# A weight stream issued from two engines instead of one

## The chip, the cores and the metric

The kernel runs on one core of a Trainium2 chip. The metric is device time in microseconds (us) of one execution. Time before the change: 2597.24 us, the median of 3 runs (2592.43 to 2603.32).

## The reference, cut to what matters

All arrays are bf16. Two branches are mixed by a gate per row: `A` is a recurrent attention with memory over 64 segments, `B` is a gated feed-forward block.

```python
# x: 2048 x 1024; 32 heads of 128; memory of 8 rows; segments of 32 rows
mem = mem0
for s in range(64):
    h = concat([mem, x[32 * s:32 * s + 32]])            # 40 rows
    q, k, v = h @ Wq, h @ Wk, h @ Wv                    # each 1024 x 4096
    scores = where(mask, q @ k.T * scale, -1e9)         # by head, 40 x 40
    o = softmax(scores) @ v
    o = o @ Wo                                          # 4096 x 1024
    mem = o[:8]                                         # goes into the next segment
    outs.append(o[8:])
a = concat(outs)
b = (gelu(x @ w_gate) * (x @ w_up)) @ w_down            # inner width 3584
g = sigmoid((x * gate_w).sum(-1))
out = g * a + (1 - g) * b
```

A segment needs the memory rows of the one before, so the 64 segments follow each other. Each uses all four attention weights, 8 MB apiece, and SBUF does not hold all of them.

## The kernel before, in words

**Recording and order.** The kernel records operations with `op(engine, function, r, w, dsem)`. Each engine (pe, act, dve, pool, sp) then runs its own operations strictly in the order in which they were recorded. `_Sched` derives the waits from what is read (`r`) and written (`w`), and `lower` turns them into semaphore waits. An operation that must wait stops its engine's queue at that point; everything recorded later on that engine stands behind it. A DMA is an operation of the engine that issues it, and it raises its own semaphore (`dsem`) when it has landed.

**First part, up to 603 us.** Branch B runs in four blocks of 512 rows; its results go to a DRAM scratch (`b_scr`). In the same time 19 pieces of 512 KB of the attention weights are rearranged in DRAM into `w_scr` (`copy_wide`), each as 128 rows of 4 KB.

**Recurrent part, the 64 segments.** Most of the attention weights stay in SBUF (`arena`), some pieces are kept in PSUM banks or in small buffers and copied back in each segment (lines 870 to 881), and 19 pieces a segment come anew from `w_scr`: the weight stream. They go through `ring`, which has 10 slots of 256 KB. A piece takes two slots, so the ring holds five blocks. Because the first segment has one block of a single slot, later blocks begin at odd slots, and each fifth block wraps around the end of the ring and is loaded by two DMAs of 256 KB.

`stream` lists the blocks in the order of their use. `stream_next` records the load of the next block, on SP. It is called by `slot_free`, which stands right behind the PE operations that use up a block: recorded there, the load waits for those matmuls, since it overwrites the slots that they read. SP does nothing else in this part.

In a segment PE projects q, k and v for two halves of the heads (line 894, eight steps a projection, four matmuls of 512 columns a step, two of the eight steps from the ring), transposes q and k (line 921), forms scores (954), transposes the probabilities (984), multiplies them by v (995) and applies the output projection (1036). Rows that can be computed ahead for four later segments run in between (795 and 1017).

ACT, in its order: it evicts q and k (`rows`, line 900), evicts rows computed ahead (`rowsx`, 809), takes the exponential of the softmax (967, behind DVE's subtraction at 965), copies v (`vt`, 914), one of the transposes (926), the attention output (`oT` and `oe`, 1003 and 1004), and at the end of a segment the output rows (`rows`, 1129). That last copy leads over one PE transpose (1137) and one DVE copy (`hT`, 1142) to the memory rows of the next segment. POOL issues the small loads and stores (x, the rows computed ahead, v rows, b, the output) from a queue of its own.

Of the kernel before, what the change touches and what calls it, by code (L numbers as in the profile page):

```python
# [26 lines left out]
class _Sched:  # L27
# [10 lines left out]
    def op(self, eng, mk, r=(), w=(), dsem=None):  # L38
        o = _Op(eng, mk, dsem)
        deps = []  # L40
        if eng == "pool" and dsem is None:
            w = [*w, ("pool",)]
        for k in r:
            deps += self.w.get(k, ())
            if k[0] == "P":
                deps += [x for x in self.r.get(k, ()) if x.eng != eng]
        for k in w:
            deps += self.w.get(k, ())
            deps += self.r.get(k, ())
        for k in r:  # L50
            self.r.setdefault(k, []).append(o)
        for k in w:
            self.w[k] = [o]
            self.r[k] = []
        seen = set()
        for d in deps:
            if d is o or id(d) in seen:
                continue
            seen.add(id(d))
            if d.eng == eng and d.dsem is None and (eng == "pe" or eng == "sp"):  # L60
                continue
            o.deps.append(d)
            d.sig = True
        self.ops.append(o)
        return o
# [63 lines left out]
def bass_gated_mix__memory_aug_recurrent_mem_tr__geglu_ffn__prompt_kernel(  # L129
# [38 lines left out]
    with ExitStack() as es:  # L168
# [54 lines left out]
        op = g.op  # L223
# [353 lines left out]
        n_str = [0]  # L577
        at = [0]

        def stream_next():  # L580
            s, u, wd = stream[n_str[0]]
            n_str[0] += 1
            sl = at[0]
            at[0] = (sl + wd) % RING
            slots = [(sl + j) % RING for j in range(wd)]
            for j in range(wd):
                slot_of[(s, u, j)] = slots[j]
            if u in wide:
                src = w_scr[wide.index(u), :, 0:wd * 1024]
            else:  # L590
                src = A_Wq[u[2] * 128:(u[2] + 1) * 128, 16 - 8 * wd if wd == 2 else 8:16, :].rearrange("p h e -> p (h e)")
            cut = min(wd, RING - sl)
            for a, b in ((0, cut), (cut, wd)):
                if a < b:
                    op("sp", lambda e, a=a, b=b: e.dma_start(
                        ring[:, slots[a]:slots[a] + b - a, :].rearrange("p a b -> p (a b)"), src[:, a * 1024:b * 1024]),
                       r=[("rp", u)], w=[("ring", y, x) for y in slots[a:b] for x in range(2)], dsem=f"ring{slots[a]}")

# [2 lines left out]
        def slot_free(k):  # L601
            free[0] += k
            while n_str[0] < len(stream) and free[0] >= stream[n_str[0]][2]:
                free[0] -= stream[n_str[0]][2]
                stream_next()
# [601 lines left out]
```

## Time and profile before

| | before |
|---|---|
| median of 3 runs | 2597.24 us |
| profiled execution | 2594.39 us |
| its span, first to last instruction | 2592.6 us |
| PE busy | 2288.7 us (88%) |
| DVE busy | 1213.1 us (47%) |
| ACT busy | 881.8 us (34%) |
| POOL busy | 546.0 us (21%) |
| mean granted TensorE clock | 0.966 |
| moved by DMA | 797.27 MB |
| of it through SP's hardware queue (q1) | 737.31 MB |
| through ACT's hardware queue (q10) | 0.06 MB |
| through POOL's software queue (q0) | 54.99 MB |
| ring loads, all issued by SP | 973 of 512 KB, 486 of 256 KB, and two from `A_Wq` |

The span is what lies between the first and the last instruction of the profiled execution, whose own time is 1.8 us longer. Busy times leave out instructions that issue DMAs, wait or branch. A share of the whole span mixes the first part, where branch B is computed, with the recurrent part, so the views by window and by wait say more on the stream than the totals do. Where a wait has several causes, the profile names the last one.

### The profile page before, as it was taken

The numbers are of one execution on the slowest core, as the hardware profiler recorded it, in microseconds if no ns is written. First come the engines' busy times: TensorE is split into PE (matmuls) and PEld (weight loads), VectorE is DVE, ScalarE is ACT, GpSimd is POOL, SyncE is SP. The second block draws the span as 40 slices with busy tenths as digits, with TensorE's granted clock in tenths as the row PEclk, the third lists the DMA queues.
The fourth block names the chain that finished last, engine by engine and source line by source line (L and its number), as shares of the span: only waits on it lengthen the run. The fifth ranks groups of instructions, "written<-read, shape, count | busy, mean of one in ns | idle before, by whom it ended". The sixth has DMA issues, their size and how long they took to land.

```text
span 2592.6 us, 77055 instructions
## 1 busy us (share of the span) xinstructions
PE 2288.7 (88%) x33919; PEld 1141.8 (44%) x33975; DVE 1213.1 (47%) x3497; ACT 881.8 (34%) x2131; POOL 546.0 (21%) x908
## 2 busy tenths in 40 slices
PE   8999999998888888888888888888888888988887
PEld 4444444444444444444444444444444444444444
DVE  5626262533444444445544444545444444455444
ACT  3314131321333333333333333333333333333332
POOL 1000003001222222222322222222222222223222
PEclk9999999999899999999999899999998999999988
DMA  8627263567999999999999999999999999999998
GB/s 286 223 75 261 75 205 97 179 247 258 331 318 343 345 348 354 355 340 369 361 357 356 339 349 336 356 323 366 354 346 335 354 335 365 345 368 357 357 344 286
DMA packets 325533, 797.27 MB, mean 308 GB/s; under 512 B 54552, under 2 KB 112232, under 8 KB 324432
## 3 DMA queue, kind: packets, MB, share of 16 engines
q1 hardware_dynamic: 282544, 737.31, 79.2%
q0 software_dynamic: 42512, 54.99, 6.8%
q8 instruction: 267, 4.37, 0.7%
q14 instruction: 66, 0.54, 0.1%
q10 hardware_dynamic: 144, 0.06, 0.0%
HBM read 764.52 MB, written 37.22 MB: 309 GB/s over the span
## 4 chain that ended last, share of the span: by engine, by line
PE 61%; DMA 26%; DVE 7%; issue 2%; ACT 2%; POOL 0%; SPq 0%; DVEq 0%; ACTq 0%
DMA ring<-w_scr 24%; PE pbb L894 10%; PE pba L894 9%; PE pbc L795 4%; PE pbb L1036 3%; PE pba L1036 3%; PE pbe L984 2%; PE pbe L921 2%; DVE ptb L989 2%; PE pbe L445 2%; PE pbh L445 2%; PE pbf L445 2%; PE pbg L445 2%; PE pbc L1017 2%; PE pbf L995 2%
## 5 line engine op out<-in xcount | busy, mean ns | idle before, releaser
L894 PE MATMUL pbb<-arena,hT 128*32 128x512 bf16 x4416 | 380.4, 399 | 9.1 <-DVE hT L1142 9.1
L894 PE MATMUL pba<-arena,hT 128*32 128x512 bf16 x4416 | 374.3, 390 | 8.8 <-DVE hT L1142 8.8
L928 DVE COPY qk<-pbe 128x512 bf16<-128x512 bf16 x192 | 132.9, 692 | 417.6 <-PE pbe L921 417.6
L967 ACT ACTIVATE pbd<-pbd 104x160 f32<-104x160 f32 x256 | 71.9, 281 | 514.3 <-DVE pbd L965 514.3
L703 POOL DMA_DIRECT2D vt<-v_scr x252 | 144.9, 577 | 335.1 <-PE pbf L995 199.5
L795 PE MATMUL pbc<-arena,xe 128*32 128x512 bf16 x2208 | 192.4, 385 | 9.7 <-DVE pn L1154 8.4
L989 DVE COPY ptb<-pbe 80x320 bf16<-80x320 bf16 x256 | 81.9, 320 | 251.5 <-PE pbe L984 251.5
L894 PE MATMUL pbb<-ring,hT 128*32 128x512 bf16 x1536 | 160.8, 407 | 29.8 <-DMA ring<-w_scr 28.9
L894 PE MATMUL pba<-ring,hT 128*32 128x512 bf16 x1542 | 157.4, 395 | 33.6 <-DMA ring<-w_scr 32.2
L894 PEld LDWEIGHTS pbb<-arena,hT 128*32 128x32 bf16 x4416 | 121.5, 100 | 120.7 <-issue 20.8
L894 PEld LDWEIGHTS pba<-arena,hT 128*32 128x32 bf16 x4416 | 119.7, 98 | 114.0 <-DVE hT L1142 14.6
L900 ACT ACTIVATE rows<-pba 128x512 bf16<-128x512 f32 x128 | 76.6, 598 | 244.5 <-PE pba L894 244.5
L1036 PE MATMUL pba<-arena,oT 128*32 128x256 bf16 x2176 | 136.0, 289 | 21.4 <-ACT oT L1003 19.0
L1036 PE MATMUL pbb<-arena,oT 128*32 128x256 bf16 x2176 | 139.9, 283 | 12.0 <-ACT oT L1003 11.7
L690 POOL DMA_DIRECT2D qkst<-qk_scr x126 | 71.8, 570 | 355.4 <-DVE qk L940 355.4
L974 DVE TENSOR_TENSOR pn<-pbd,rr 104x256 bf16<-104x256 f32 (+1 forms) x512 | 142.3, 319 | 8.8
L1036 PE MATMUL pba<-ring,oT 128*32 128x256 bf16 x1792 | 117.0, 284 | 29.4 <-DMA ring<-w_scr 28.1
L1003 ACT ACTIVATE oT<-pbf 128x256 bf16<-128x256 f32 x256 | 97.7, 382 | 131.4 <-PE pbf L995 131.4
L900 ACT ACTIVATE rows<-pbb 128x512 bf16<-128x512 f32 x128 | 76.6, 598 | 190.4 <-PE pbb L894 190.4
L1036 PE MATMUL pbb<-ring,oT 128*32 128x256 bf16 x1792 | 123.2, 280 | 15.3 <-DMA ring<-w_scr 13.1
L968 DVE TENSOR_REDUCE rs<-pbd 104x4 f32<-104x160 f32 x256 | 82.9, 324 | 88.9 <-ACT pbd L967 88.9
L961 DVE SCALAR_TENSOR_TENSOR pbd<-pbd,mask 104x160 f32<-104x160 f32 x256 | 85.2, 333 | 76.0 <-PE pbd L954 76.0
(245 smaller groups left out, 4257.7 us busy)
## 6 DMA issues: line engine op xcount, KB each, us to landing
ring<-w_scr SPq DMA_DIRECT2D x973, 512.0 KB, 6.3
ring<-w_scr SPq DMA_DIRECT2D x486, 256.0 KB, 5.9
arena<-in_B_w_gate_dram SPq DMA_DIRECT2D x28, 1024.0 KB, 5.4
arena<-in_B_w_up_dram SPq DMA_DIRECT2D x28, 1024.0 KB, 7.8
qkst<-qk_scr POOLq DMA_DIRECT2D x126, 64.0 KB, 5.2
qk_scr<-rowsx POOLq DMA_DIRECT2D x60, 128.0 KB, 5.2
arena<-in_B_w_down_dram SPq DMA_DIRECT2D x7, 1024.0 KB, 12.3
arena<-in_A_Wk_dram SPq DMA_DIRECT2D x6, 1024.0 KB, 6.6
```

Source lines behind the costliest of these rows:

```text
L445: ins = e.matmul(PB[bank][:, :], lhsT=wv[:, kc, col:col + 128], rhs=xb[:, kc, :], start=(kc == 0), stop=(kc == KC - 1))
L703: op("pool", lambda e: e.dma_start(vt[2 * SEG:KEYS, par, :], src), r=[("vscr", s // GR, h)], w=[("vte", par), ("vte", par, 0)], dsem="vte% ...
L795: ins = e.matmul(PB[B_X][32 * gq:32 * gq + 32, :], lhsT=xe[:, us[-1], :], rhs=us[gq // 2][0][gq % 2], start=(n == 0), stop=(n == KC - 1), ...
L894: ins = e.matmul(PB[bank][32 * gq:32 * gq + 32, :], lhsT=hT[:, kc, :], rhs=us[gq // 2][0][gq % 2], start=(x == 0), stop=(x == KC - 1), ski ...
L900: op("act", lambda e: e.activation(rows[:, :], PB[bank][:, :], ACTF.Copy), r=[P(bank)], w=[("rows",)])
L928: op("dve", lambda e: e.tensor_copy(qk[:, m, :, 0:SEG, :], src), r=[P(B_T)], w=[("qk", m)])
L961: op("dve", lambda e: e.scalar_tensor_tensor(out=sv, in0=sv, scalar=scale, in1=mask[0:104, None, :].to_broadcast([104, 4, L]), op0=ALU.mul ...
L968: op("dve", lambda e: e.tensor_reduce(rsv, sv, AX.X, ALU.add), r=[P(B_S)], w=[("rs",)])
L974: op("dve", lambda e, c0=c0, k0=k0, n=n: e.tensor_tensor(out=pn[0:104, :, c0:c0 + 2 * n].rearrange("p i (two c) -> p i two c", two=2), in0 ...
L989: op("dve", lambda e: e.tensor_copy(ptb[0:KEYS, :, :, :], src), r=[P(B_PT)], w=[("ptb",)] + first)
L1003: op("act", lambda e: e.activation(dst, src[:, :, :, 0:SEG], ACTF.Copy), r=[P(B_PV)], w=[("oT", o % 2)])
L1036: ins = e.matmul(PB[B_O][32 * q:32 * q + 32, 0:256], lhsT=oT[:, o % 2, k, :], rhs=u[q // 2][:, (q % 2) * 256:(q % 2 + 1) * 256], start=(o ...
```

## The change

One line is added and one changed in `stream_next`. From the second segment on (`s > 0`), a block whose number in the stream is odd is issued by ACT (`nc.scalar`), an even one by SP. `n_str[0]` has been raised by one before this line, so blocks count from one. Both DMAs of a split block are issued by the same engine. The waits, the slots, the order in which the loads are recorded and the semaphores that tell of their landing stay; the loads of ACT take their places in ACT's own order, right behind the operations recorded before them.

```diff
             cut = min(wd, RING - sl)
+            eng = "act" if s > 0 and n_str[0] % 2 else "sp"
             for a, b in ((0, cut), (cut, wd)):
                 if a < b:
-                    op("sp", lambda e, a=a, b=b: e.dma_start(
+                    op(eng, lambda e, a=a, b=b: e.dma_start(
                         ring[:, slots[a]:slots[a] + b - a, :].rearrange("p a b -> p (a b)"), src[:, a * 1024:b * 1024]),
                        r=[("rp", u)], w=[("ring", y, x) for y in slots[a:b] for x in range(2)], dsem=f"ring{slots[a]}")
```

Line numbers in the text are those of the kernel before; from line 594 on the changed kernel's are higher by one.

## The prediction

> **What bounds the kernel now.** I read the windows view first, to see which resources are full in the recurrent stage, where all the moved transfers lie. Its columns are: window, length, then busy time and instructions of PE, PEld, DVE, ACT and POOL, the granted TensorE clock, the DMA share and GB/s.
>
> ```profile
> 1000.00:1500.00 500.00, 432.14 (x8098) 223.74 (x8099) 239.29 (x791) 183.40 (x454) 130.74 (x213) 0.98 0.98 353
> 1500.00:2000.00 500.00, 428.96 (x7880) 219.48 (x7872) 237.88 (x789) 181.05 (x449) 126.65 (x207) 0.96 0.97 347
> 2000.00:2500.00 500.00, 430.05 (x7964) 220.57 (x7966) 239.75 (x792) 183.36 (x455) 126.38 (x207) 0.97 0.99 354
> ```
>
> Two things are nearly full at once: the DMA engines carry packets for 0.97 to 0.99 of the time, and PE is busy for 0.86. ACT is busy for 0.37, so it has room. Line 1142 runs 50 times from 1006.3 to 2495.8 us: 49 steps, 30.4 us a segment. The change acts on 63 of the 64 segments, some 1,915 us.
>
> Next the waits of PE, whole span (total us, times, longest):
>
> ```profile
> PE pba L894 <- DMA ring<-w_scr: 32.2, 51, 1.8
> PE pbb L894 <- DMA ring<-w_scr: 28.9, 52, 2.3
> PE pba L1036 <- DMA ring<-w_scr: 28.1, 39, 1.8
> PE pbe L1137 <- ACT rows L1129: 23.5, 48, 0.5
> PE pba L1036 <- ACT oT L1003: 19.0, 37, 1.0
> ...
> PE pbb L1036 <- DMA ring<-w_scr: 13.1, 19, 1.7
> PE pbb L1036 <- ACT oT L1003: 11.7, 32, 1.0
> ```
>
> The ring costs PE 102.3 us in short waits, and two ACT copies that every segment must pass cost 54.2 us. A later ring block lengthens the first kind, a later ACT the second. The page's chain has the ring at 24% of the span, in pieces like the 6.42 and 6.63 us here:
>
> ```profile
> 1509.81 6.42 DMA ring<-w_scr
> ...
> 1519.70 0.39 ACT rows L1129
> ...
> 1523.72 0.12 SPq L595
> 1523.85 0.04 issue
> 1523.89 6.63 DMA ring<-w_scr
> ```
>
> The loop to see: PE frees a block, SP issues its refill within 0.12 us, it lands 6.6 us later, and PE stands there. Last, the issuing line itself (ns min/median/max) and its landing:
>
> ```profile
> L595 SPq DMA_DIRECT2D ring<-w_scr x1459: 319/320/2487, 514.5 to 2577.4; - x183
> ...
> DMA to landing us min/median/max: 2.5/6.2/9.1
> ```
>
> A 512 KB block at 350 GB/s takes 1.5 us, so a landing time of 6.2 us is a queue of some four. Counting issues not yet landed in the trace from 700 to 2500 us, no ring transfer at all is open for only 0.1 us. The queue never runs dry; what varies is its depth.
>
> **The change, part by part.** By the program's order, 717 of the 1,461 ring DMAs go from SP to ACT (479 of 512 KB, 238 of 256 KB: 598 blocks); nothing changes in the order of PE, DVE and POOL, and no byte is added. A moved DMA keeps its wait for the PE matmul that frees its slots, but behind it on ACT stand now the evictions, the exponentials and the copies; in front of it stands whatever ACT has not finished.
>
> *SP loses 717 issues.* SP is in nobody's way afterwards; it saves nothing but its own back-to-back issues: the second half of a split block took 0.53 us on average against 0.35 for a whole block, 243 times. The data are queued 6 us ahead, so this is worth nothing; if that cover were gone it would be 243 x 0.18 = 44 us.
>
> *Term A, late issues.* For each moved DMA I compared its issue on SP with the end of the ACT operation that will stand before it. For 48% ACT ends later; over all 717 the delay averages 0.31 us, at most 1.74 us (behind the vt copies of line 914). Averaged over both queues that is 0.31 x 717/1461 = 0.15 us a DMA, and at 24 DMAs in 30.4 us, 0.12 DMAs fewer in flight. What a DMA in flight is worth I take from the trace in bins of 1 us: with 3 to 4 ring DMAs open the engines moved 334 GB/s (316 bins), with 4 to 5 357 (582), with 5 to 6 366 (739): 16 GB/s for each. So 0.12 x 16 = 1.9 GB/s of 350, 0.5% of 1,915 us: 10 us. The ends are 0 (the queue covers it) and 20 (with 2 to 3 open the rate was 270 GB/s in 106 bins; the mean slope over all four bins is 32).
>
> *Term B, two queues side by side.* In one queue blocks land in the order of use, median 1.28 us apart. In two, a block and its successor can be moved together and land together; one then lies unused in the ring while PE works on the other, on average half a block, 0.6 DMAs, for all the time that the two queues are in step. Upper end: 0.6 x 16 = 9.6 GB/s, 2.7% of 1,915, 52 us. Lower end: 0, when they alternate exactly, as evenly spaced issues would have them; it could lie below 0 only if two queues move more bytes, a rival below. Blocks are freed one by one, which is nearer to alternation, but each fifth is split into two small DMAs, which disturbs it: I take a quarter, 13 us.
>
> The Trainium skill (DMA: Bandwidth & Descriptors, Queues, rings and completion order) says that each DMA engine takes turns between the queues it has work for. That would be the mechanism of the upper end: 52 us instead of 13, and a sum of 2669 instead of 2630; the trace of before, with one hardware queue in this stage, cannot show it for two.
>
> *Term C, ACT's own work behind an issue.* I let each moved DMA hold ACT for 0.38 us, the mean of SP's issues, from the later of PE's release and the end of the ACT operation before it, and looked how far it pushes the next one. The sum is 56 us: line 900 22.4, line 1003 16.9, line 1129 13.7, line 914 3.0. ACT's only DMAs in this trace are at the end and small, two in 0.97 us:
>
> ```profile
> 2585.65 0.97 ACTq L1150 DMA_DIRECT2D out_dram<-bo  x2
> ```
>
> so 0.49 us is not excluded, and 0.32 neither. Line 900 is followed by several units of PE work before its result is transposed, so it has cover. Lines 1003 and 1129 are what PE waits for above: 30.6 us at most. While PE stands, the ring fills, so part comes back from the 102 us of ring waits. I take a third, 10 us; ends 0 and 31.
>
> *POOL's queue* now shares the engines with two queues. Its tightest loads landed 2.1 us (hT) and 2.7 us (qkst) before use at the least, against a landing time of 5.4 and 5.2 us; a slower turn up to 40% is covered. Nothing taken.
>
> **Sum.** 10 + 13 + 10 = 33 us on the profiled execution, which took 2594.4 us (span 2592.6): 2627.4. The median of the runs, 2597.2, is 2.8 higher: 2630. With all terms at 0 it is 2597, at their upper ends 2597 + 103 = 2700.
>
> **The rivals.**
> *No change, 2597.* The DMA share of 0.97 to 0.99 says that the bytes set the pace, and they stay. If a queue of four and a ring of five blocks swallow the 0.31 us, and the copies' delay is given back as shorter ring waits, nothing is left. For it: the delay is small against 6.2 us. Against it: rate and depth go together in the bins above. The Trainium skill (DMA: Bandwidth & Descriptors, Issuing engines are not separate DMA queues) states that DMAs issued from several engines end on the same 16 DMA engines, and that only issue time is saved. By that the next rival could give nothing, and 2597 would be the best there is; the trace of before shows no second stream to hold against it.
>
> *Faster, about 2570.* The DMA engines' packets fill 0.975 of the stage; the missing 2.5% is 48 us. A second queue could offer a DMA engine work while the first has none ready. Filled half, that is 24 us: 2573; wholly, 2549. It decides from the point where the two queues' rate passes today's 350 GB/s by more than A to C take, about 2%. For it: at 5 to 6 open DMAs the rate is still rising. Against it: PE can only get back what it waits for, 102 us, and already with 5 open no engine is free on average (16.05 packets under way at a time).
>
> *Much slower, about 2675.* An issue can hold its engine: some of SP's lasted up to 2.49 us, always right behind another issue; the excess over 0.32 us averages 0.06 us. On SP nobody waits behind it; on ACT it is 717 x 0.06 = 44 us more in front of exponentials and copies: 2630 + 44 = 2674. Against it: two queues each hold half as many open DMAs, and fewer of ACT's issues come back to back.
>
> **How the numbers follow.** About 0.5% of this time, 13 us, is what a measurement can tell from no change. Forecast with terms A to C 0.46, much slower 0.14, no change 0.22, faster 0.18. The first two lie above 2610: slower 0.60. The range takes in the forecast's bounds and most of the other cases: 2572, the half-filled gap, to 2690, just over the much slower case.
>
> **What would show it.** Right: ring waits of PE above 102 us and a DMA share below 0.97 in the three windows; waits for lines 1003 and 1129 above 54 us; ring issues on ACT near 0.35 us; landing times that scatter more than 2.5 to 9.1 us. If ring waits stay at 102 and only the ACT waits grow, term C alone is real. If GB/s in the windows rises above 354, the faster rival is it. If ACT's issues last over 0.7 us by the dozen, the much slower one. The forecast is wrong if PE's waits for the ring fall.

## The result and the profile after

The changed kernel takes 2730.5 us (median of 4 runs), the kernel before 2594.8 us beside it: ratio 1.0526, 95% interval 1.0487 to 1.0566. It is 5.3% slower, some 136 us, where 33 were forecast. The profiled execution took 2736.2 us, its span is 2734.4 us, 141.8 more than before.

The windows of the recurrent part, columns as in the view of before (window, length, PE, PEld, DVE, ACT, POOL, clock, DMA share, GB/s):

```profile
1000.00:1500.00 500.00, 417.82 (x7418) 212.15 (x7418) 222.97 (x739) 169.92 (x419) 119.62 (x194) 0.92 0.94 326
1500.00:2000.00 500.00, 413.64 (x7454) 212.59 (x7450) 223.75 (x743) 171.46 (x422) 120.54 (x196) 0.93 0.93 326
2000.00:2500.00 500.00, 419.92 (x7372) 214.09 (x7376) 220.40 (x728) 169.36 (x418) 119.37 (x194) 0.90 0.92 323
```

The DMA engines are less busy (0.92 to 0.94, from 0.97 to 0.99) and move 325 GB/s, not 350. The granted clock falls from 0.96 to 0.98 down to 0.90 to 0.93. PE does about 7% fewer matmuls in the same time.

PE's waits over the whole span (total us, times, longest):

```profile
PE pba L895 <- DMA ring<-w_scr: 50.8, 54, 2.5
PE pbb L895 <- DMA ring<-w_scr: 49.1, 54, 2.3
PE pba L1037 <- DMA ring<-w_scr: 45.6, 37, 4.0
PE pbe L1138 <- ACT rows L1130: 34.3, 61, 1.5
PE pbb L1037 <- DMA ring<-w_scr: 31.9, 22, 3.2
PE pba L1037 <- ACT oT L1004: 25.8, 61, 1.2
...
PE pbb L1037 <- ACT oT L1004: 11.7, 32, 1.0
```

The ring now costs 177.4 us (before 102.3), in about as many waits (167, before 161), which are longer. The two ACT copies cost 71.8 (before 54.2). The issuing line:

```profile
L596 SPq DMA_DIRECT2D ring<-w_scr x742: 319/320/1920, 512.1 to 2719.2; - x186
L596 ACTq DMA_DIRECT2D ring<-w_scr x717: 325/326/1397, 646.8 to 2717.9; - x180
...
DMA to landing us min/median/max: 2.7/6.0/10.2
```

An issue takes ACT 326 ns in the median, about as long as it takes SP (320). The landing time has hardly moved in the median, but its range is wider.

The recurrent part alone, from its first matmul (line 894, 895 in the changed kernel) to the end, before and after, in the columns of the windows view:

```profile
604.68:2592.60 1987.91, 1698.19 (x31151) 869.76 (x31150) 936.40 (x3093) 710.08 (x1757) 501.10 (x819) 0.96 0.96 345
602.32:2734.40 2132.08, 1764.10 (x31151) 896.97 (x31150) 936.35 (x3093) 713.70 (x1757) 502.59 (x819) 0.91 0.92 321
```

It is 144 us longer, the first part 2.4 us shorter. PE is busy 66 us longer for the same number of matmuls, so they run slower. Its ring waits grew by 75 us, all its waits for ACT by 19 (the two copies by 18), and the rest of its idle time shrank by 16: 66 + 75 + 19 - 16 = 144.

### The profile page after: what moved, and what is told of

Its sections match the earlier page's. It is cut to its first block, busy times and chain, and to the rows that moved or that the text cites. A ratio compares the mean times of both kernels' runs of the same rounds, so it can differ in the third digit from the quotient of the medians.

```text
span 2734.4 us, 77111 instructions
## 1 busy us (share of the span) xinstructions
PE 2356.3 (86%) x33975; PEld 1168.8 (43%) x33975; DVE 1213.1 (44%) x3497; ACT 885.4 (32%) x2131; POOL 547.7 (20%) x908
## 4 chain that ended last, share of the span: by engine, by line
PE 59%; DMA 29%; DVE 6%; ACT 2%; issue 2%; ACTq 0%; POOL 0%; SPq 0%; DVEq 0%
DMA ring<-w_scr 28%; PE pbb L895 10%; PE pba L895 9%; PE pbb L1037 4%; PE pbc L796 4%; PE pba L1037 3%; PE pbe L985 2%; PE pbe L922 2%; PE pbf L445 2%; PE pbg L445 2%; PE pbh L445 2%; PE pbe L445 2%; DVE ptb L990 2%; PE pbc L1018 2%; PE pbb L445 2%
## 5 line engine op out<-in xcount | busy, mean ns | idle before, releaser
L895 PE MATMUL pbb<-arena,hT 128*32 128x512 bf16 x4416 | 392.3, 411 | 9.1 <-DVE hT L1143 9.1
L895 PE MATMUL pba<-arena,hT 128*32 128x512 bf16 x4416 | 387.7, 402 | 8.8 <-DVE hT L1143 8.8
L1037 PE MATMUL pba<-arena,oT 128*32 128x256 bf16 x2176 | 143.8, 304 | 28.5 <-ACT oT L1004 25.8
L1037 PE MATMUL pba<-ring,oT 128*32 128x256 bf16 x1792 | 124.2, 298 | 45.8 <-DMA ring<-w_scr 45.6
L1037 PE MATMUL pbb<-ring,oT 128*32 128x256 bf16 x1792 | 132.0, 296 | 33.3 <-DMA ring<-w_scr 31.9
L1037 PE MATMUL pbb<-arena,oT 128*32 128x256 bf16 x2176 | 149.9, 300 | 12.4 <-ACT oT L1004 11.7
L833 POOL DMA_DIRECT2D qk_scr<-rowsx x60 | 47.8, 797 | 350.6 <-DVE rowsx L830 340.7
```

The source lines that it names most:

```text
L895: ins = e.matmul(PB[bank][32 * gq:32 * gq + 32, :], lhsT=hT[:, kc, :], rhs=us[gq // 2][0][gq % 2], start=(x == 0), stop=(x == KC - 1), ski ...
L1037: ins = e.matmul(PB[B_O][32 * q:32 * q + 32, 0:256], lhsT=oT[:, o % 2, k, :], rhs=u[q // 2][:, (q % 2) * 256:(q % 2 + 1) * 256], start=(o ...
```

## The experiments

Three theories stood at the start. **T1**: two queues loaded at once are the cause. **T2**: issues on ACT come late, behind ACT's work. **T3**: the issues hold up ACT's own copies. All edits are to the changed kernel unless the text says otherwise; ratios are to the kernel before, with the 95% interval.

### Whole segments in turn

```diff
-            eng = "act" if s > 0 and n_str[0] % 2 else "sp"
+            eng = "act" if s % 2 else "sp"
```

> Whole segments alternate: odd segments load all their ring blocks from ACT, even ones from SP. 729 DMAs move, about as many as in the change (717), and each stands in ACT's order behind the same kinds of work, but the two queues hold transfers together only where two segments meet. If two queues side by side are the cause (T1): 2600 to 2625, most of the loss gone. If late issues behind ACT's work are it (T2): 2700 to 2760, as in the change. If ACT's own copies held up by the issues are it (T3): also 2700 to 2760.

Measured: 2611.2 us, ratio 1.0083 (1.0047 to 1.0120). As T1 said. 729 DMAs on ACT cost 0.8% when the queues do not run side by side; PE's ring waits are 99.0 us, about those of before (102.3), and only the waits for the copies grew:

```profile
PE pbe L1138 <- ACT rows L1130: 36.8, 48, 1.2
PE pba L895 <- DMA ring<-w_scr: 31.5, 47, 1.7
PE pba L1037 <- ACT oT L1004: 26.9, 55, 1.4
PE pba L1037 <- DMA ring<-w_scr: 25.9, 45, 1.3
PE pbb L1037 <- DMA ring<-w_scr: 24.3, 37, 1.8
PE pbb L895 <- DMA ring<-w_scr: 17.3, 35, 1.9
```

### Prompt places and late places

```diff
+        PROMPT = (("k", 0, 7), ("k", 1, 6), ("o", 0, 4), ("o", 2, 4), ("q", 0, 6), ("q", 1, 6),
+                  ("q", 1, 7), ("v", 0, 6), ("v", 0, 7), ("v", 1, 6))
-            eng = "act" if s > 0 and n_str[0] % 2 else "sp"
+            eng = "act" if s > 0 and u in PROMPT else "sp"
```

The second kernel has `not in` for `in`.

> Of the 19 blocks of a segment, the ten whose place in ACT's order is early enough in the trace of before (ACT idle when PE frees the slots) go to ACT: 756 DMAs. T1: 2690 to 2750, since both queues still carry transfers together all the time. T2: 2600 to 2620, since these issues are not late. T3: 2610 to 2650.

> The other nine blocks go to ACT: those where ACT, in the trace of before, was still at work 0.2 to 1.4 us after PE had freed the slots; 680 DMAs. T1: 2690 to 2750, like the ten prompt ones. T2: above 2750, all of the late places and twice as often as in the change. T3: 2650 to 2720.

Measured: prompt 2665.0 us, 1.0274 (1.0217 to 1.0332); late 2657.1 us, 1.0248 (1.0214 to 1.0281). Whether ACT is in time makes no difference: T2 falls. Late lies in T3's range, prompt above it. Both stay below T1's 2690, though: ten of the blocks in one, nine in the other, cost half of what every second block costs. In both the stream changes engine 10 times a segment, in the change 19 times.

### ACT's issues without the stream

SP issues every ring block; ACT issues a small DMA that carries no weights (below: the empty DMAs) at each place with the same waits.

```diff
-            eng = "act" if s > 0 and n_str[0] % 2 else "sp"
+            eng = "sp"
+            mark = s > 0 and n_str[0] % 2
...
-                    op(eng, lambda e, a=a, b=b: e.dma_start(
+                    o = op(eng, lambda e, a=a, b=b: e.dma_start(
...
+                    if mark:
+                        n_dz[0] += 1
+                        z = n_dz[0] % 8
+                        t = op("act", lambda e, z=z: e.dma_start(dz[:, z * 4:z * 4 + 4], w_scr[0, :, 0:4]),
+                               w=[("dz", z)], dsem=f"dz{z}")
+                        t.deps += [d for d in o.deps if d.eng == "pe" and d not in t.deps]
```

> SP issues every ring block, as before; ACT issues 717 DMAs of 1 KB into a small buffer that nobody reads, at the places where the change has its loads and with the same waits for PE. Only ACT's own cost of issuing is left. T1 and T2: 2600 to 2625 (term C of the prediction was 10 us, its upper end 31). T3: 2680 or more.

Measured: 2614.8 us, 1.0075 (1.0045 to 1.0106), some 20 us: term C, and about all that T3 explains.

T1 is left, and it can mean two things. **S**: two loaded queues lower the rate, however the blocks are dealt. **O**: neighbouring blocks, dealt to two queues, land unevenly, and the ring stands emptier.

### All blocks from ACT

```diff
-            eng = "act" if s > 0 and n_str[0] % 2 else "sp"
+            eng = "act" if s > 0 else "sp"
```

> Every ring load from the second segment on is issued by ACT, 1434 of them: one queue, the order of use, and twice the ACT cost of the change with every late place taken. S and O: twice the cost of the kernel with the empty DMAs (which was 0.75%), 2625 to 2650. If late issues mattered after all: above 2700.

Measured: 2617.1 us, 1.0090 (1.0053 to 1.0127). With every issue on ACT, every late place taken and one queue, the loss is no larger than that of the empty DMAs. The doubling that was expected did not come: PE's waits for the two copies grew to 92.6 us (71.7 with the empty DMAs), but its ring waits fell to 78.7 (99.4). Late issues cost nothing that can be seen.

### Two from ACT, two from SP

```diff
-            eng = "act" if s > 0 and n_str[0] % 2 else "sp"
+            eng = "act" if s > 0 and n_str[0] // 2 % 2 else "sp"
```

> Two blocks from ACT, two from SP, in turn: the same half of the stream is moved, both queues are loaded nearly all the time, and the engine changes half as often. S: 2700 to 2735, as in the change. If the loss counts the changes of engine (half of it in the kernels with ten and nine blocks moved, which change 10 times a segment and not 19): 2655 to 2675. O, with whole pairs overtaking each other: above 2740.

Measured: 2678.7 us, 1.0311 (1.0275 to 1.0348). None of the three hit; it lies 4 us above the count of changes (9.5 a segment) and clearly below the two others. What the changes of engine do shows in the landing times in the traces, block by block from segment 2 on. "Hold" is the mean time from a block's landing in order to the issue of the block that takes its slots; "in flight" is the mean number of blocks issued and not yet landed, from 700 to 2,500 us; "landing" is the mean time from a block's issue to its landing.

| kernel | changes a segment | ratio | spread of landing gaps (sd, us) | gaps under 0.8 us | hold, us | in flight | landing, us |
|---|---|---|---|---|---|---|---|
| before | 0 | 1 | 0.51 | 0 | 1.73 | 3.92 | 6.31 |
| empty DMAs on ACT | 0 | 1.0075 | 0.49 | 0 | 1.68 | 3.97 | 6.43 |
| all from ACT | 0 | 1.0090 | 0.50 | 0 | 1.95 | 3.79 | 6.16 |
| segments in turn | 1 | 1.0083 | 0.60 | 3% | 1.86 | 3.86 | 6.29 |
| late places | 10 | 1.0248 | 0.97 | 13% | 1.95 | 3.82 | 6.33 |
| prompt places | 10 | 1.0274 | 0.94 | 14% | 2.02 | 3.79 | 6.37 |
| two and two | 9.5 | 1.0311 | 1.04 | 14% | 2.20 | 3.70 | 6.26 |
| the change | 19 | 1.0526 | 1.05 | 16% | 2.36 | 3.63 | 6.26 |

In one queue no block ever lands within 0.8 us of its predecessor. In two, neighbours bunch, and a long gap stands ahead of a bunch (with the change 2.9 us on average, where all gaps average 1.7). A landed block lies longer, its refill goes out later, and fewer blocks are in flight: 3.92 before, 3.63 with the change.

No single column explains the losses, though. Two and two bunches nearly as much as the change and loses 3.1%, not 5.3%. All from ACT and prompt places have the same 3.79 blocks in flight and lose 0.9% and 2.7%; in the one queue the blocks then land sooner than before, in the two they do not. Why they do not is not shown.

### Halves of a block, by rows

The edits of this section and the next are to the kernel before. Each ring load from the second segment on is two DMAs, rows 0 to 63 and 64 to 127; in half_sp both from SP, in half_act the second from ACT.

```diff
+                    if s == 0:
...
+                        continue
+                    for x in range(2):
+                        op(("sp", "act")[x], lambda e, a=a, b=b, x=x: e.dma_start(
+                            ring[64 * x:64 * x + 64, slots[a]:slots[a] + b - a, :].rearrange("p a b -> p (a b)"),
+                            src[64 * x:64 * x + 64, a * 1024:b * 1024]),
+                           r=[("rp", u)], w=[("ring", y, x) for y in slots[a:b]], dsem=f"ring{('', 'b')[x]}{slots[a]}")
```

> Control for half_act: from the second segment on each ring load is split by rows into 0 to 63 and 64 to 127, both issued by SP; the packets stay the same size. Both theories: 2595 to 2625, one queue, twice the issues, one wait more for PE.

> As half_sp, but rows 64 to 127 come from ACT: both queues carry transfers side by side all the time, yet each serves the blocks in the order of use, so that no block waits for half a queue of a later one. ACT's own cost is that of act_all, which issues as many DMAs. If uneven landing of neighbouring blocks is the cause (O): no slower than act_all, within 1%. If two loaded queues cost rate however the blocks are dealt (S): slower than act_all by 3 to 5%, some 80 to 120 us.

Measured: half_sp 3368.5 us, 1.2986 (1.2924 to 1.3049); half_act 3248.7 us, 1.2538 (1.2467 to 1.2608). The control itself lost 30%, with a single queue: from 1,000 to 2,500 us a packet of 4 KB took 265 ns on average, in the kernel before 177. It is not the doubled number of DMAs: the control of the next section has that too and loses 1.3%. Loads of 64 rows are slow here by themselves, so this pair says nothing on whole blocks in two queues. That half_act was 3.5% faster than its control was not followed up.

### Halves of a block, by slot

The same question with all 128 rows: every slot has a DMA of its own, and in col_act the second slot's comes from ACT.

```diff
+                    for x in range(a, b) if s > 0 else ():
+                        op(("sp", "act")[x], lambda e, x=x: e.dma_start(ring[:, slots[x], :], src[:, x * 1024:(x + 1) * 1024]),
+                           r=[("rp", u)], w=[("ring", slots[x], y) for y in range(2)], dsem=f"ring{slots[x]}")
+                    if s > 0:
+                        continue
```

> Control for col_act: from the second segment on every ring slot is loaded by a DMA of its own (128 rows of 2 KB), both of a block issued by SP. Both theories: 2600 to 2680; half blocks are already part of the stream, and their packets take 84 ns against 162 for 4 KB.

> As col_sp, but the second slot of every block comes from ACT: two queues loaded side by side all the time, each in the order of use, the two halves of one block next to each other. If uneven landing of neighbouring blocks is the cause (O): col_sp plus the cost of ACT issues, 1% at most. If two loaded queues lower the rate as such (S): col_sp plus 3 to 5%.

Measured: col_sp 2630.0 us, 1.0128 (1.0097 to 1.0158); col_act 2643.0 us, 1.0174 (1.0138 to 1.0211). Two loaded queues, in the order of use, cost 0.5% over the control, and the intervals overlap. That is no more than ACT's share by the empty DMAs, 0.75%; S, with its 3 to 5%, falls in the kernel.

### The stream alone

These kernels leave out all computation and load 1,218 blocks, each issue waiting for the block `DEPTH` places before it. Each kernel of this section ran once.

```python
for n in range(N):                       # N = 1218; each engine takes its own n
    if n >= DEPTH:
        e.wait_ge(sems[(n - DEPTH) % SLOTS], 16 * ((n - DEPTH) // SLOTS + 1))
    e.dma_start(ring[:, n % SLOTS, :], src[n % n_src, :, :]).then_inc(sems[n % SLOTS], 16)
```

> No computation: 1,218 blocks of 512 KB are loaded from B_w_down into SBUF by SP, each issue waiting for the landing of the fourth block before it; then the output is written from what was loaded. It measures the rate of one queue by itself. Both theories: 340 to 370 GB/s while it streams.

> The same stream, even blocks from SP and odd ones from ACT, each waiting for the fourth block before it, which is its own queue's last but one. PE and the order of use play no part. O: the rate of bench_one within 1%. S: 3 to 5% below it.

Measured: one queue 1582.5 us, two queues 2238.6 us, with four blocks open in both. The rate of the one queue lies above the expected 340 to 370 GB/s. With two it is 30% lower (the time 41% longer), where S had said 3 to 5% and O at most 1%: both missed. The DMA part of the page, one queue first, then two:

```profile
DMA  9999999999999999999999999999999999999999
...
DMA packets 177706, 642.94 MB, mean 407 GB/s; under 512 B 19744, under 2 KB 19744, under 8 KB 177696
...
ring<-in_B_w_down_dram SPq DMA_DIRECT2D x1218, 512.0 KB, 5.1
```

```profile
DMA  8777878778778778778778778778777778778777
...
DMA packets 177706, 642.94 MB, mean 287 GB/s; under 512 B 19744, under 2 KB 19744, under 8 KB 177696
...
ring<-in_B_w_down_dram SPq DMA_DIRECT2D x609, 512.0 KB, 7.3
ring<-in_B_w_down_dram ACTq DMA_DIRECT2D x609, 512.0 KB, 7.3
```

The engines stand idle for a fifth of the time (a share of 0.79 from 200 to 1,300 us), although a block is issued as soon as the fourth before it has landed. A block's semaphore is raised 16 times as the block lands; the first and the last of these come 1.06 us apart in the median with one queue, 3.59 us with two. A block counts as landed with the last of them; that engines which were done earlier have nothing left by then would fit, and is not shown. Is the rate itself lower, or is it only too few blocks for the spread?

> As bench_two, but each issue waits for the eighth block before it and not the fourth: four blocks open in each queue. If taking turns lowers the rate itself: still near 290 GB/s, 2,240 us. If engines run dry while a block waits for the last of them: 370 to 410 GB/s, 1,580 to 1,740 us.

> As bench_one (depth of four blocks), but the first half of each row's 4 KB comes from SP and the second from ACT, so both queues are loaded all the time and hold the blocks in the same order. If taking turns lowers the rate: near 290 GB/s. If the order of blocks between the queues is what costs: 370 to 410 GB/s.

> As bench_two with five blocks open, as many as the kernel's ring holds; each issue then waits for a block of the other queue. If a block waits for the last of 16 engines while others run dry, five open blocks leave part of the loss of four: 310 to 390 GB/s, 1,660 to 2,080 us. If the loss at four was only two queues of two running in step: 400 GB/s and more.

> As bench_one with three blocks open in SP's single queue. If a single queue keeps all engines on the same block, three blocks are nearly enough: 380 to 410 GB/s. If depth alone had made bench_two slow, three blocks in one queue would fall to 300 GB/s or less.

Measured: two queues with eight blocks open 1580.3 us, with five 1580.9 us; halves in two queues with four open 1673.5 us (385 GB/s; its 2 KB packets take 88 ns, more than half of the 163 for 4 KB); one queue with three open 2037.3 us. For three open in one queue, and five in two:

```profile
DMA  9999889898999899899999998988899999989998
...
DMA packets 177706, 642.94 MB, mean 316 GB/s; under 512 B 19744, under 2 KB 19744, under 8 KB 177696
```

```profile
DMA packets 177706, 642.94 MB, mean 407 GB/s; under 512 B 19744, under 2 KB 19744, under 8 KB 177696
...
ring<-in_B_w_down_dram SPq DMA_DIRECT2D x609, 512.0 KB, 6.4
ring<-in_B_w_down_dram ACTq DMA_DIRECT2D x609, 512.0 KB, 6.4
```

So two loaded queues cost no rate as such: with five open they move 409 GB/s from 200 to 1,300 us. Four blocks are enough for one queue and not for two. One block short, either falls off: 316 GB/s in one queue of three, 287 in two of two. My expectation that a single queue would nearly manage with three was wrong. For five, the figure that hit is that of two queues of two running in step (with four open each issue waits for a block of its own queue, with five for one of the other). So these runs do not tell whether two queues need more depth or only must not be paired off two and two.

### One block less, one queue

The kernel before, with four ring blocks:

```diff
-    RING = 10
+    RING = 8
```

> The kernel before with a ring of eight slots, four blocks instead of five; one queue. If the change is slow because two queues use up about one block of depth: 2680 to 2790, with ring waits of PE near the change's 177 us and a lower granted clock. If depth has little to do with it: 2595 to 2650.

Measured: 2798.5 us, 1.0783 (1.0725 to 1.0841), 8 us beyond the upper end expected. PE's waits and windows:

```profile
PE pba L1036 <- DMA ring<-w_scr: 63.0, 78, 2.6
PE pba L894 <- DMA ring<-w_scr: 59.1, 94, 2.7
PE pbb L894 <- DMA ring<-w_scr: 56.0, 84, 2.4
PE pbb L1036 <- DMA ring<-w_scr: 48.7, 73, 2.2
PE pbe L1137 <- ACT rows L1129: 23.4, 48, 0.5
```

```profile
1500.00:2000.00 500.00, 410.95 (x7216) 203.60 (x7214) 214.78 (x710) 165.30 (x407) 116.85 (x190) 0.93 0.92 317
```

The picture is that of the change with one queue: 226.8 us of ring waits, a DMA share of 0.92, a clock of 0.93. PE waits for ACT's copies as before. A block of depth is worth 7.8% of this kernel, some 203 us; the change, less ACT's 20 us, lost 116, as much as 0.57 of a block. Counted as in the table, this kernel has 3.17 blocks in flight, 0.75 fewer than before, and they land after 5.64 us; the change has 0.29 fewer, or 0.39 of that, and they land after 6.26 us. So fewer blocks in flight are, by this price, some 79 of the 116 us; the rest goes with landing times that do not shorten.

### The small loads in SP's queue

The kernel before, with the loads of x, rows computed ahead, v rows and b issued by SP instead of POOL.

```diff
-            op("pool", lambda e: e.dma_start(hT[:, :, :].rearrange("p kc c -> p (kc c)"),
+            op("sp" if s > 1 else "pool", lambda e: e.dma_start(hT[:, :, :].rearrange("p kc c -> p (kc c)"),
```

and the same for `qkst`, `vt` and `bo`.

> The kernel before with one more edit: the small loads of the recurrent part (x, the rows computed ahead, v rows, b; 16 to 64 KB) go from POOL's queue to SP's, where they stand in one line with the ring. If a second loaded queue upsets the landing of ring blocks here too: 2560 to 2590. If not, or if their waits on SP hold up the ring: 2595 to 2640.

Measured: 2607.1 us, 1.0058 (1.0028 to 1.0088). Nothing is won. The spread of the landing gaps is 0.52 us, as before (0.51), so there is no sign that the small loads in a second queue hurt the ring. No kernel tried beats the one before.

## Why the prediction was wrong, point by point

**Direction and mechanism** were right: slower, by ring waits above 102 us, a DMA share below 0.97, longer waits for the two copies, and a wider range of landing times, each as the last part of the prediction listed them.

**Term B was mis-sized, and it is the step that failed.** The prediction took a quarter of "on average half a block", 13 us, with 52 as its end. The runs give 5.26% less the 0.75% of the empty DMAs, some 116 us. Both of its factors were too small. The price: 16 GB/s for each DMA in flight, read from bins of the trace of before, made half a block 52 us, where half of ring_four's 203 is 102. The bins compare moments within one execution; taking a block away for good costs far more. The amount: a quarter of 0.6 DMAs is 0.15, and the change has 0.36 fewer in flight (4.21, before 4.57, from 700 to 2,500 us). "Freed one by one, nearer to alternation" does not hold, since 16% of the neighbours bunch. The 1.28 us that the prediction gives between landings is the median of DMAs, halves included; whole blocks land 1.43 us apart. Nothing in the sum rests on it.

The Trainium skill (DMA: Bandwidth & Descriptors, Queues, rings and completion order) says that each engine takes turns between queues. The stream alone agrees that two queues are served together: with five blocks open both have packets under way in 98% of the time, 8.2 of each on average. Which engine carries a packet the trace does not say. The same page of the Trainium skill (section Issuing engines are not separate DMA queues) says that issuing from several engines only saves issue time. The runs agree in that nothing was gained; here it cost 5.3%, and the measurement decides.

**Left out: the matmuls' own time.** The same matmuls took PE 66 us longer in the recurrent part, and the sum had no term for it; it is part of the 116 us. The granted clock went from 0.966 to 0.932. The traces' clock records are at one half in 29 stretches before, 180 us in all, and in 50 after, 375 us; otherwise they are at full clock. In the 3.4 us ahead of such a stretch PE was idle for 0.50 of the time before and 0.56 after (medians), in the other pieces of 3.4 us at full clock for 0.04. half_sp (0.861) and ring_four (0.938) show the same fall with one queue, so it follows PE's stalls and not the queues. One long stall is not needed: half_sp has 129 stretches at one half and four idle pieces of PE over 3.4 us. No run varied the clock by itself.

**Term A** (10 us) was nothing that can be seen: prompt and late places cost the same, and all blocks from ACT no more than the empty DMAs. **Term C** (10 us) was 20, inside its ends of 0 and 31. **POOL's queue** at nothing: no wait of PE for one of its loads is among the larger ones after the change.

**The rivals.** No change: refuted. Faster: refuted, the rate fell from 350 to 325 GB/s. Both read a DMA share near one as nearly full. The stream alone moves 408 GB/s at a share of 1.03, its 4 KB packets taking 163 ns where they take 177 in the kernel before; it reads another tensor and has no other traffic, but it shows that the share's distance from one does not measure what is left. Much slower by issues that hold ACT: its 2675 was nearer than the forecast, but for the wrong reason; issues on ACT took 326 ns in the median and 1.40 us at most.

**Still open:** why blocks in two queues land in bunches, and no sooner when fewer are in flight. That the DMA engines serve the two queues in different orders would fit the stream with four blocks open, where the raises of a block's semaphore spread over 3.59 us and not 1.06, but the trace does not name a packet's engine. In the kernel itself that spread grew less: from 2.1 to 2.2 us in the median, from 3.23 to 3.89 at the 95th percentile.

## What to carry to other kernels

Where a ring of few blocks feeds PE and PE waits for it, keep its loads in one queue: blocks dealt over two queues landed in bunches here, and cost as much as about half a block of depth. To price depth, take a block away in a run; a correlation of rate and depth inside one trace set it at about half. When PE will wait more, count the lower clock on top of the waits.

## What the runs showed of the hardware that was not expected

- One queue of 512 KB loads (128 rows of 4 KB) reaches 408 GB/s with four open and 316 with three; two queues 287 with four and 409 with five (one run each).
- Loads of 64 rows are slow: in half_sp, with the same row length, packets of 4 KB took 265 ns on average against 177, and the kernel moved 248 GB/s from 700 to 2,500 us with nine ring DMAs open on average.
- PE's clock went to one half after pieces of 3.4 us in which PE was idle for about half of the time (median 0.50 before, 0.56 after), for 180 us before and 375 us after.
- A DMA issued by ACT costs ACT 0.33 us, and 717 or 1,436 of them cost this kernel the same 0.8 to 0.9%.
